# Key features as weights: two heads a product in 64-column array tiles

## The chip, the cores and the metric

The kernel runs on one core of a Trainium2 chip. The metric is the time of one execution on the device in microseconds, as the median of several runs. Before the change it is 507.56 us (three runs, 507.46 to 507.66).

## What is computed

The reference mixes two branches over one input x of 2048 rows and 512 columns:

```python
g = _sigmoid((x * gate_w).sum(-1, keepdims=True))
a = _A_ref(x, A_wqkv, A_w_phi, A_wo)
b = _B_ref(x, B_w1, B_b1, B_w2, B_b2)
return g * a + (1 - g) * b
```

Branch B is a dense layer of 1792 hidden columns with a squared ReLU. Branch A is linear attention with 32 heads of 16 columns:

```python
pq = jnp.einsum("bhsd,hdf->bhsf", q, w_phi)
pk = jnp.einsum("bhsd,hdf->bhsf", k, w_phi)
phi_q = jnp.concatenate([_softmax(pq, axis=-1), _softmax(-pq, axis=-1)], axis=-1)
phi_k = jnp.concatenate([_softmax(pk, axis=-1), _softmax(-pk, axis=-1)], axis=-1)
kv = jnp.einsum("bhsf,bhsd->bhfd", phi_k, v)
z  = jnp.einsum("bhsf->bhf", phi_k)
num = jnp.einsum("bhqf,bhfd->bhqd", phi_q, kv)
den = jnp.einsum("bhqf,bhf->bhq", phi_q, z)[..., None] + 1e-6
o = num / den
```

For each head the 2048 rows of 32 key features (16 of a softmax and 16 of the softmax of the negative) are multiplied with 16 columns of values. That gives a 32 x 16 matrix kv and a sum z of 32 numbers a head.

## The kernel before

**Order of the work.** The program goes through a list of 56 hidden steps: two sweeps over the hidden columns, in each four blocks of 512 rows, in each seven groups of 128 hidden columns. One step multiplies up (tile u), squares on ScalarE, and multiplies down (tile d). The attention is hung between these steps: `at(slot, f)` puts a piece of work at a place written out by hand, and `run(slot)` issues it there. Each engine works through its own instructions in order, so the slots set the order on TensorE and, with a few priorities (`high_priority`), on the others. Most products are done as three float32r products of high and low parts (`mm3`); the products of this change are plain float32.

**Keys and values.** In the first sweep, `tiles_fold` multiplies the key weights with w_phi (PSUM tiles fold), turns the result with four VectorE transposes (line 194, tile turned) and spreads it with 16 ScalarE copies (line 198) into the tiles raw. From these, `joint` makes the operands of a block product that yields keys and values of two row chunks (a pair) at a time, in the PSUM tiles pX and pY (lines 653 to 655). The key part becomes the features phi (tile e or tmp, 32 heads x 32 features); the value part goes into vext, where each head has 17 columns: 16 values and a one. The column of ones makes the sum z beside kv.

**The key-value products.** For each chunk of 128 rows `kv_chunk` (lines 319 to 326) issues 32 products, one a head. The weights are the 17 columns of vext, the moving side the 32 features of the head. Head 8j + g is written to the 17 partitions from 32j on, in the 32 columns from 32g on, of the one PSUM tile kvps: four array tiles of 32 columns work side by side. All 16 chunks add up in kvps. Each of eight pairs issues its two chunks in one go (`kv`, line 710).

**The end of the sums.** `kv_done` copies the four groups of 17 partitions into a zeroed tile (line 751). The row of ones lies in partitions 16, 48, 80 and 112 of it; one DMA writes these four rows to memory (zrow, line 752), two read them back into every partition (z, line 755). `kv_blocks` transposes the tile on VectorE (line 760) and copies the blocks into kvb (line 764), the weights of the numerator products num (line 385). The tile z is read by GpSimd in `q_exps` (line 333) for the denominator. The PSUM bank of kvps is handed back at the end of `kv_done`.

The queries follow in the second sweep: their weights are folded (foldq, line 152), q is projected and turned to features, and num and the output product att come after.

Of the kernel before, what the change touches and what calls it, by code (L numbers as in the profile page):

```python
# [7 lines left out]
F32 = mybir.dt.float32  # L8
F32R = mybir.dt.float32r
AF = mybir.ActivationFunctionType  # L10
# [5 lines left out]
P = 128  # L16
S, D, H, DH, F = 2048, 512, 32, 16, 1792
NK = D // P
SB = 512
NB = S // SB  # L20
# [5 lines left out]
NG = 8  # L26
VW = DH + 1
# [7 lines left out]
def tile_gated_mix(ctx: ExitStack, tc: tile.TileContext, xT, xn, wqT, wkT, wphi, wv, wo, w1, b1, w2, b2, gw, out):  # L35
    nc = tc.nc
# [6 lines left out]
    work = pool("work", 2)  # L43
    small = pool("small", 3)
    dram = pool("dram", 1, space=DRAM)
    ps_d = pool("ps_d", NC, space=PSUM)
    ps_a, ps_b, ps_e, ps_f = (pool(f"ps_{i}", 1, space=PSUM) for i in "abef")
# [5 lines left out]
    def bank(name):  # L53
        p = banks[0]
        used(p)
        return p.tile([P, 512], F32, tag="s", name=name)
# [63 lines left out]
    st, up_w, down_w = {}, {}, {}  # L120
# [6 lines left out]
    kvb = const.tile([P, NG, 2 * DH], F32, name="kvb")  # L127
# [1 line left out]
    nc.gpsimd.tensor_tensor(kvb, kvb, kvb, ALU.add)  # L129
    part = dram.tile([NB * NC, P, D], F32, name="part")  # L130
    wkeep = dram.tile([len(KEPT), 2, P, 2 * D], F32, name="wkeep")
    zrow = dram.tile([2 * D], F32, name="zrow")
    vext = [hold.tile([P, H * VW], F32, tag="vz", name=f"vext{i}") for i in range(NV)]
    heads = lambda v: v.rearrange("p (h v) -> p h v", v=VW)
    for v in vext:
# [39 lines left out]
    def tiles_fold(loaded):  # L175
        wph, *t = loaded
        pss = [bank(f"fold{r}") for r in range(4)]

        def mm(g, r, c):
            rows, cols = slice(32 * r, 32 * r + 32), slice(32 * c, 32 * c + 32)  # L180
            return nc.tensor.matmul(pss[r][cols, g * P:(g + 1) * P],
                                    wph[rows, g * P + 32 * r:g * P + 32 * r + 32],
                                    t[g][rows, :].rearrange("p (k c q) -> p k c q", c=4, q=32)[:, :, c, :],
                                    start=True, stop=True, skip_group_check=True)

        last = None
        for x in [(g, r, c) for g in range(NK) for c in range(4) for r in range(4)]:
            with tc.issue_after(last.ins) if last else nullcontext():
                last = mm(*x)
        for half in range(2):  # L190
            tb = work.tile([P, 2, 4, NK, 32], F32, tag="tb", name="turned", bufs=2)
            for r in range(2):
                with tc.high_priority(offset=AHEAD):
                    st["turned"] = nc.vector.transpose(tb[:, r].rearrange("p g k q -> p (g k q)"), pss[2 * half + r])
            for k in range(NK):
                dst = st["raw"][k].rearrange("p (h z g r f) -> p h z g r f", h=2, z=2, g=2, r=4)
                for h in range(2):
                    nc.scalar.activation(dst[:, h, 0, :, 2 * half:2 * half + 2],
                                         tb[:, :, 2 * h:2 * h + 2, k].rearrange("p r g q -> p g r q"), AF.Copy)

    def operand(i, j, src, slot=None, ehi=None, elo=None):
        if i in HELD:
# [114 lines left out]


    def kv_chunk(first, last, kvps, phi, v):
        for g in range(NG):  # L320
            for j in range(4):
                h = NG * j + g
                mm = nc.tensor.matmul(kvps[32 * j:32 * j + VW, 32 * g:32 * g + 32], v[:, h * VW:(h + 1) * VW],
                                      phi[:, 32 * h:32 * h + 32], start=(first and g == 0), stop=last,
                                      skip_group_check=True)
        return mm

    def q_exps(n, ps):
# [268 lines left out]
    LASTP = len(ROWS) - 1  # L597
# [59 lines left out]
    def pair_steps(p, s):  # L657
        b, c = ROWS[p]
        n, m = b * NC + c, b * NC + c + 2
        v = {}  # L660

        def place(t, half, src, other=None):
            i = 2 * p + (t == m)
            if ("e", t) not in v:
                v["e", t] = e_tile("tmp" if i % NV == NV - 1 else "e")
                v["v", t] = vext[i % NV]
            hs = slice(16 * half, 16 * half + 16)
            to = (v["e", t][:, hs, 0, :], heads(v["v", t])[:, hs, :DH])
            for o, cols in zip(to, halves):
                of = lambda z: z[:, cols].rearrange("p (h f) -> p h f", f=DH)  # L670
                if other is None:
                    read = nc.scalar.activation(o, of(src), AF.Copy)
                else:
                    read = nc.vector.tensor_tensor(o, of(other), of(src), ALU.add)
            return read

        def run(i):
            first, other = i in (1, 2, 7), "Y" if i in (2, 7, 4) else "X"
            if i == 1:
                if p == 0:  # L680
                    banks.remove(ps_e)
                v["X"] = ps_e.tile([P, 512], F32, tag="s", name="pX")
            elif first:
                v["bank"] = banks[0]
                v["Y"] = bank("pY")
            elif i == 4:
                used(v["bank"])
            block(v[other], p, i, first)
            with tc.high_priority(offset=AHEAD), again(p, i, 0):
                if i in (1, 6, 5):  # L690
                    v[i] = st["tmp"][0][:, 512 * (i == 6):512 * (i == 6) + 512]
                    read = nc.scalar.activation(v[i], v["X"], AF.Copy)  # L692
                elif i == 7:
                    return
                else:
                    t, half, u = {2: (n, 0, 1), 3: (n, 1, None), 4: (m, 0, 6)}[i]
                    read = place(t, half, v[other], v.get(u))
            with tc.issue_after(read.ins):
                again(p, i, 1)

        def place7():
            with tc.high_priority(offset=AHEAD):
                place(m, 1, v["Y"], v[5])

        def phi(t):
            e3, r = exps(e=v["e", t])
            with tc.high_priority(offset=AHEAD):
                v["phi", t] = scaled(e3, r)

        def kv():  # L710
            if p == 0:
                st["kv"] = ps_b.tile([P, 2 * P], F32, tag="s", name="kvps")
            later = kv_chunk(p == 0, False, st["kv"], v["phi", m], v["v", m])
            with tc.issue_after(later.ins):
                kv_chunk(False, p == LASTP, st["kv"], v["phi", n], v["v", n])

        at(s - 2 - (p > 0), sums_load, p)
        if p == 0:
            at(s - 2, sums_add, p)
        at(s - 1.5 if p else s - 0.5, sums, p)  # L720
        for off, i in zip((0, 1, 1.5, 2, 2.5, 3, 4), (1, 2, 6, 5, 7, 3, 4)):
            at(s + off, run, i)
        if p == LASTP:
            at(s + 4, banks.append, ps_e)
        at(s + 3, place7)
        at(s + 3, phi, n)
        at(s + 4, phi, m)
        at(s + 7.5 + (p == LASTP) / 2, kv)

    def do_q(b, n, c):  # L730
# [10 lines left out]

    def kv_room():
        t = row()
        st["kvs"], st["kvt"] = t[:, :2 * P], t[:, 2 * P:]
        nc.gpsimd.memset(st["kvs"], 0.0)

    def kv_done():
        kvps, kvs = st["kv"], st["kvs"]
        for j in range(4):
            s = slice(32 * j, 32 * j + VW)  # L750
            nc.vector.tensor_copy(kvs[s, :], kvps[s, :])
        nc.sync.dma_start(zrow.rearrange("(j x) -> j x", j=4), kvs[DH::32, :])
        for half in range(2):
            z = hold.tile([P, H * VW], F32, tag="vz", name=f"z{half}")[:, :D]
            nc.sync.dma_start(z, zrow[half * D:(half + 1) * D].partition_broadcast(P))
            zbc.append(z.rearrange("p (h f) -> p h f", f=DH))
        banks.append(ps_b)

    def kv_blocks():
        nc.vector.transpose(st["kvt"], st["kvs"])  # L760
        kt = st["kvt"].rearrange("p (g v) -> p g v", v=32)
        for j in range(4):
            s = slice(32 * j, 32 * j + 32)
            nc.vector.tensor_copy(kvb[s, :, DH * (j % 2):DH * (j % 2 + 1)], kt[s, :, :DH])

    def finish(n, c):
        ps = attended(st["o", n // 2], n % 2, st["wb"])
# [14 lines left out]
    SL = 2 * NFH  # L782
    steps = {}

    def at(slot, f, *a):
        steps.setdefault(int(2 * slot) / 2, []).append(lambda: f(*a))
# [10 lines left out]
    for b in range(NB):  # L797
        for c in range(NC):
            s = b * SL + 2.5 * c - 1 if b > 1 else 17.5 + c / 2 if b else max(5.5, 3.5 + 2 * c)
# [5 lines left out]
        s, late = ((4, 2), (19.5, 1), (22, 2.5), (36, 2))[b]  # L805
# [15 lines left out]
            at(slot + 1.5, ffn_split, nm, NFH + i)  # L821
    at(51, kv_room)
    at(NB * SL - 1, kv_done)
    at(NB * SL + 4, kv_blocks)

    for p in range(NB * NC // 2):
        n, s = 2 * p, 56.5 + 6 * p
        q, late = divmod(n, NC)[0], p == NB * NC // 2 - 1  # L830
# [13 lines left out]
    hid, last = {}, len(work_list) - 1  # L844
# [25 lines left out]
    for t, (sw, b, i) in enumerate(work_list):  # L870
# [17 lines left out]
        for c in range(NC):  # L888
            n = b * NC + c
# [9 lines left out]
            dst = part[n] if sw == 0 else out[n * P:(n + 1) * P, :]  # L899
# [52 lines left out]
```

## Time and profile before

| what | value |
|---|---|
| median of three runs | 507.56 us |
| profiled execution | 507.18 us |
| its span | 505.4 us |
| TensorE busy | 500.7 us, 3520 products |
| TensorE weight loads | 406.1 us |
| VectorE, ScalarE, GpSimd busy | 407.0, 256.6, 87.3 us |
| moved by DMA | 76.13 MB |

The span runs from the first to the last instruction of the profiled execution; 1.8 us of its time lie around it. PE is TensorE, PEld its weight loads, which overlap PE; DVE is VectorE, ACT ScalarE, POOL GpSimd, SP the engine that issues most DMAs. A row of a group of instructions begins with the line of the kernel, the engine and the operation, then the output tile and the inputs. For a product follow the size of the weights (rows*columns) and the size of the moving side. A busy share of PE is no measure of its peak: consecutive products overlap, and their ends are modelled.

### The profile page before, as it was taken

What the parts mean: (1) busy time and instruction counts of PE and PEld (TensorE: products, weight loads), DVE (VectorE), ACT (ScalarE), POOL (GpSimd) and SP (SyncE); (2) the same over time, 40 slices, a digit from 0 to 9 for tenths busy, and PEclk for the clock granted to TensorE, in tenths of its full rate; (3) what the DMA queues carried; (4) which work ended last, traced back from release to release, by engine and by line L of the source; (5) the groups of instructions that cost most, each with busy time, mean ns of one, the idle gap of its engine ahead of it and who ended that gap; (6) DMA issues with size and microseconds to landing.
All of it is one profiled execution on the core that took longest, in us unless ns stands there. A gap on an engine that the chain in (4) does not pass through costs nothing.

```text
span 505.4 us, 9354 instructions
## 1 busy us (share of the span) xinstructions
PE 500.7 (99%) x3520; PEld 406.1 (80%) x3520; DVE 407.0 (81%) x680; ACT 256.6 (51%) x458; POOL 87.3 (17%) x102
## 2 busy tenths in 40 slices
PE   9999999999999999999999999999999999999997
PEld 5878888788888888888888878788787878788776
DVE  5569957988695979796998989897979796897724
ACT  4887655565253474454674744454455353333540
POOL 1000151204410035000013040212222221112200
PEclk9999999999999999999999999999999999999999
DMA  8858587756854578771265311325112231041112
GB/s 261 291 196 273 198 305 225 237 190 234 285 184 165 183 223 294 265 228 65 83 211 209 98 49 48 99 64 150 49 31 90 71 86 43 8 131 57 38 27 83
DMA packets 45829, 76.13 MB, mean 151 GB/s; under 512 B 6868, under 2 KB 23000, under 8 KB 45784
## 3 DMA queue, kind: packets, MB, share of 16 engines
q1 hardware_dynamic: 36072, 41.78, 26.6%
q10 hardware_dynamic: 6768, 23.79, 13.7%
q0 software_dynamic: 2944, 9.96, 5.5%
q8 instruction: 28, 0.46, 0.4%
q14 instruction: 17, 0.14, 0.1%
HBM read 57.68 MB, written 11.54 MB: 137 GB/s over the span
## 4 chain that ended last, share of the span: by engine, by line
PE 98%; DMA 1%; DVE 0%; issue 0%
PE d L76 10%; PE d L77 10%; PE d L78 10%; PE u L76 10%; PE u L77 9%; PE u L78 9%; PE pX L653 3%; PE q L77 3%; PE att L77 3%; PE att L78 3%; PE att L76 3%; PE q L78 3%; PE q L76 3%; PE pX L655 3%; PE pX L654 3%; PE pY L655 2%
## 5 line engine op out<-in xcount | busy, mean ns | idle before, releaser
L421 ACT ACTIVATE r<-u,b1c 128x512 f32<-128x512 f32 x56 | 38.5, 687 | 122.9 <-PE u L78 121.2
L76 PE MATMUL d<-w2h,hh 128*128 128x512 f32 x222 | 86.9, 391 | 0.0
L77 PE MATMUL d<-w2l,hh 128*128 128x512 f32 x222 | 86.4, 389 | 0.0
L78 PE MATMUL d<-w2h,hl 128*128 128x512 f32 x222 | 86.4, 389 | 0.0
L76 PE MATMUL u<-xh,w1h 128*128 128x512 f32 x212 | 83.6, 394 | 0.0
L77 PE MATMUL u<-xl,w1h 128*128 128x512 f32 x212 | 82.6, 390 | 0.0
L78 PE MATMUL u<-xh,w1l 128*128 128x512 f32 x212 | 82.5, 389 | 0.0
L333 POOL TENSOR_TENSOR ez<-e,z 128x512 f32<-128x512 f32 x32 | 42.9, 1360 | 165.0 <-ACT e L309 165.0
L66 DVE TENSOR_TENSOR hl<-r,hh 128x512 fp32r<-128x512 f32 x56 | 37.8, 676 | 24.3 <-ACT hh L63 24.1
L76 PEld LDWEIGHTS d<-w2h,hh 128*128 128x128 f32 x222 | 41.7, 188 | 9.2 <-issue 0.6
L76 PEld LDWEIGHTS u<-xh,w1h 128*128 128x128 f32 x212 | 39.8, 188 | 11.1 <-issue 2.9
L78 PEld LDWEIGHTS d<-w2h,hl 128*128 128x128 f32 x222 | 41.7, 188 | 8.7
L77 PEld LDWEIGHTS d<-w2l,hh 128*128 128x128 f32 x222 | 41.7, 188 | 8.5
L78 PEld LDWEIGHTS u<-xh,w1l 128*128 128x128 f32 x212 | 39.8, 188 | 8.6 <-DVE w1l L66 0.2
L77 PEld LDWEIGHTS u<-xl,w1h 128*128 128x128 f32 x212 | 39.8, 188 | 7.9
L309 ACT ACTIVATE e<-e 128x1024 f32<-128x1024 f32 x27 | 28.6, 1059 | 26.5 <-DVE e L307 26.1
L291 DVE TENSOR_REDUCE sm<-e 128x64 f32<-128x1024 f32 x27 | 32.8, 1215 | 10.8 <-ACT e L309 10.8
L63 ACT ACTIVATE hh<-r 128x512 fp32r<-128x512 f32 x56 | 35.2, 628 | 1.1
L423 ACT ACTIVATE r<-r 128x512 f32<-128x512 f32 x56 | 34.9, 624 | 0.7
L692 ACT ACTIVATE tmp<-pX 128x512 f32<-128x512 f32 x24 | 14.4, 598 | 30.6 <-PE pX L655 27.0
L374 ACT ACTIVATE phiT<-tb 32x256 f32<-32x256 f32 x64 | 26.4, 412 | 5.8 <-DVE tb L359 4.9
L343 DVE TENSOR_REDUCE dz<-ez 128x64 f32<-128x1024 f32 x16 | 19.4, 1212 | 11.7 <-POOL ez L333 11.7
(182 smaller groups left out, 984.2 us busy)
## 6 DMA issues: line engine op xcount, KB each, us to landing
sloto<-wkeep ACTq DMA_DIRECT2D x30, 512.0 KB, 4.6
in<-in_xT SPq DMA_DIRECT2D x42, 256.0 KB, 4.4
slotez<-wkeep ACTq DMA_DIRECT2D x15, 512.0 KB, 5.0
phiT<-tb SPq DMA_DIRECT2D x192, 32.0 KB, 1.8
in<-in_w SPq DMA_DIRECT2D x23, 256.0 KB, 3.3
part<-row POOLq DMA_DIRECT2D x16, 256.0 KB, 5.5
row<-part SPq DMA_DIRECT2D x16, 256.0 KB, 3.0
out<-row SPq DMA_DIRECT2D x15, 256.0 KB, 2.2
```

The costliest lines, as they stand in the source:

```text
L63: i = nc.scalar.activation(hi, src, AF.Copy)
L66: st["lo"] = elo.tensor_tensor(lo, src, hi.bitcast(F32), ALU.subtract)
L76: nc.tensor.matmul(o, ah[:, sa], bh[:, sb], start=first, stop=False)
L77: nc.tensor.matmul(o, ah[:, sa], bl[:, sb], start=False, stop=False)
L78: return nc.tensor.matmul(o, al[:, sa], bh[:, sb], start=False, stop=last)
L291: nc.vector.tensor_reduce(sm, e3, AX.X, ALU.add)
L309: nc.scalar.activation(ef, ef, AF.Exp)
L333: nc.gpsimd.tensor_tensor(ez[:, hs, :], e3[:, hs, :], zbc[half], ALU.mult)
L374: nc.scalar.activation(dst, src, AF.Copy)
L421: st["relu"] = nc.scalar.activation(r, ps, AF.Relu, bias=b1c[:, fc:fc + 1])
L423: nc.scalar.activation(r, r, AF.Square)
L655: nc.tensor.matmul(ps, l, wh, start=False, stop=j == 1, skip_group_check=True)
```

## The change

The two sides of the key-value product are exchanged, and two heads share a product. The weights are now 64 columns: the features of two heads. The moving side is the extended values of the same two heads, 2 x 17 columns. The product has four blocks, of which the two with features and values of the same head are used. It is written to 64 partitions of kvps, so that two array tiles of 64 columns take turns.

```diff
     def kv_chunk(first, last, kvps, phi, v):
+        fs = phi.rearrange("p (q g f) -> q g p f", q=2, g=NG)
+        vs = v.rearrange("p (q a g f) -> q g p a f", q=2, a=2, g=NG)
         for g in range(NG):
-            for j in range(4):
-                h = NG * j + g
-                mm = nc.tensor.matmul(kvps[32 * j:32 * j + VW, 32 * g:32 * g + 32], v[:, h * VW:(h + 1) * VW],
-                                      phi[:, 32 * h:32 * h + 32], start=(first and g == 0), stop=last,
-                                      skip_group_check=True)
+            for q in range(2):
+                mm = nc.tensor.matmul(kvps[64 * q:64 * q + 64, 2 * VW * g:2 * VW * (g + 1)], fs[q, g], vs[q, g],
+                                      start=(first and g == 0), stop=last, skip_group_check=True)
         return mm
```

For this the features of the two heads must lie side by side. The order of the key columns is changed where the folded weights are spread; the values stay where they were:

```diff
-            tb = work.tile([P, 2, 4, NK, 32], F32, tag="tb", name="turned", bufs=2)
+            tb = work.tile([P, NK, 4, 2, 32], F32, tag="tb", name="turned", bufs=2)
             for r in range(2):
                 with tc.high_priority(offset=AHEAD):
-                    st["turned"] = nc.vector.transpose(tb[:, r].rearrange("p g k q -> p (g k q)"), pss[2 * half + r])
+                    st["turned"] = nc.vector.transpose(tb[:, :, :, r].rearrange("p k g q -> p g k q"),
+                                                       pss[2 * half + r].rearrange("p (g k q) -> p g k q", g=4, k=NK))
             for k in range(NK):
-                dst = st["raw"][k].rearrange("p (h z g r f) -> p h z g r f", h=2, z=2, g=2, r=4)
+                dst = st["raw"][k].rearrange("p (h z i a d) -> p h z a i d", h=2, z=2, i=NG, a=2)
                 for h in range(2):
-                    nc.scalar.activation(dst[:, h, 0, :, 2 * half:2 * half + 2],
-                                         tb[:, :, 2 * h:2 * h + 2, k].rearrange("p r g q -> p g r q"), AF.Copy)
+                    nc.scalar.activation(dst[:, h, 0, :, 4 * half:4 * half + 4],
+                                         tb[:, k, 2 * h:2 * h + 2].rearrange("p a r (i d) -> p a (r i) d", i=2),
+                                         AF.Copy)
```

The sums now have the features on the partitions, as kvb needs them. They are copied straight from PSUM into the blocks, and only the column of sums, 8 of 32 columns, is transposed on its way to zrow; `kv_blocks` is gone:

```diff
     def kv_done():
-        kvps, kvs = st["kv"], st["kvs"]
-        for j in range(4):
-            s = slice(32 * j, 32 * j + VW)
-            nc.vector.tensor_copy(kvs[s, :], kvps[s, :])
-        nc.sync.dma_start(zrow.rearrange("(j x) -> j x", j=4), kvs[DH::32, :])
+        kv = st["kv"]
+        blocks = [(slice(32 * j, 32 * j + 32), j % 2) for j in range(4)]
+        for s, a in blocks:
+            nc.vector.tensor_copy(st["z"][s, :NG], kv[s, :, a, DH])
+        nc.vector.transpose(st["zt"], st["z"])
+        nc.sync.dma_start(zrow.rearrange("(p f) -> p f", f=32), st["zt"])
+        for s, a in blocks:
+            nc.vector.tensor_copy(kvb[s, :, DH * a:DH * (a + 1)], kv[s, :, a, :DH])
+        zr = zrow.rearrange("(j g f) -> j (g f)", j=4, f=32)
         for half in range(2):
             z = hold.tile([P, H * VW], F32, tag="vz", name=f"z{half}")[:, :D]
-            nc.sync.dma_start(z, zrow[half * D:(half + 1) * D].partition_broadcast(P))
+            nc.sync.dma_start(z.rearrange("p (j x) -> p j x", j=2),
+                              zr[2 * half:2 * half + 2, :32 * NG].partition_broadcast(P))
             zbc.append(z.rearrange("p (h f) -> p h f", f=DH))
         banks.append(ps_b)
-
-    def kv_blocks():
-        nc.vector.transpose(st["kvt"], st["kvs"])
-        kt = st["kvt"].rearrange("p (g v) -> p g v", v=32)
-        for j in range(4):
-            s = slice(32 * j, 32 * j + 32)
-            nc.vector.tensor_copy(kvb[s, :, DH * (j % 2):DH * (j % 2 + 1)], kt[s, :, :DH])
```

The rest follows from it: kvps is declared as 8 x 2 x 17 columns, zrow grows from 1024 to 4096 numbers, and the zeroed tile shrinks from 256 to 32 columns.

More of the change, by code (lines that the diff above doesn't have):

```diff
@@ L131, in tile_gated_mix @@
     wkeep = dram.tile([len(KEPT), 2, P, 2 * D], F32, name="wkeep")
-    zrow = dram.tile([2 * D], F32, name="zrow")
+    zrow = dram.tile([P * 32], F32, name="zrow")
     vext = [hold.tile([P, H * VW], F32, tag="vz", name=f"vext{i}") for i in range(NV)]
@@ L711, in kv @@
             if p == 0:
-                st["kv"] = ps_b.tile([P, 2 * P], F32, tag="s", name="kvps")
-            later = kv_chunk(p == 0, False, st["kv"], v["phi", m], v["v", m])
+                st["kv"] = ps_b.tile([P, NG, 2, VW], F32, tag="s", name="kvps")
+            out = st["kv"].rearrange("p g a v -> p (g a v)")
+            later = kv_chunk(p == 0, False, out, v["phi", m], v["v", m])
             with tc.issue_after(later.ins):
-                kv_chunk(False, p == LASTP, st["kv"], v["phi", n], v["v", n])
+                kv_chunk(False, p == LASTP, out, v["phi", n], v["v", n])
         at(s - 2 - (p > 0), sums_load, p)
@@ L743, in kv_room @@
         t = row()
-        st["kvs"], st["kvt"] = t[:, :2 * P], t[:, 2 * P:]
-        nc.gpsimd.memset(st["kvs"], 0.0)
+        st["z"], st["zt"] = t[:, :32], t[:, 32:64]
+        nc.gpsimd.memset(st["z"], 0.0)
     def kv_done():
-        kvps, kvs = st["kv"], st["kvs"]
-        for j in range(4):
-            s = slice(32 * j, 32 * j + VW)
-            nc.vector.tensor_copy(kvs[s, :], kvps[s, :])
-        nc.sync.dma_start(zrow.rearrange("(j x) -> j x", j=4), kvs[DH::32, :])
+        kv = st["kv"]
[7 more added lines that the diff above has]
+        zr = zrow.rearrange("(j g f) -> j (g f)", j=4, f=32)
         for half in range(2):
             z = hold.tile([P, H * VW], F32, tag="vz", name=f"z{half}")[:, :D]
-            nc.sync.dma_start(z, zrow[half * D:(half + 1) * D].partition_broadcast(P))
+            nc.sync.dma_start(z.rearrange("p (j x) -> p j x", j=2),
+                              zr[2 * half:2 * half + 2, :32 * NG].partition_broadcast(P))
             zbc.append(z.rearrange("p (h f) -> p h f", f=DH))
         banks.append(ps_b)
-    def kv_blocks():
-        nc.vector.transpose(st["kvt"], st["kvs"])
-        kt = st["kvt"].rearrange("p (g v) -> p g v", v=32)
-        for j in range(4):
-            s = slice(32 * j, 32 * j + 32)
-            nc.vector.tensor_copy(kvb[s, :, DH * (j % 2):DH * (j % 2 + 1)], kt[s, :, :DH])
     def finish(n, c):
@@ L823, in tile_gated_mix @@
     at(NB * SL - 1, kv_done)
-    at(NB * SL + 4, kv_blocks)
     for p in range(NB * NC // 2):
```

## The prediction

> **What bounds the kernel now.** I read the page first: the share of each engine, the slices and the chain that ended last.
>
> ```profile
> span 505.4 us, 9354 instructions
> ...
> PE 500.7 (99%) x3520; PEld 406.1 (80%) x3520; DVE 407.0 (81%) x680; ACT 256.6 (51%) x458; POOL 87.3 (17%) x102
> ...
> PE   9999999999999999999999999999999999999997
> ...
> PEclk9999999999999999999999999999999999999999
> ...
> PE 98%; DMA 1%; DVE 0%; issue 0%
> ```
>
> PE is busy in 500.7 of 505.4 us, no slice of it is open, its clock is granted in full, and 98% of the chain that ended last lies on it. The waits of PE are the second view; this is all of it:
>
> ```profile
> PE warm L497 <- DVE zeros L491: 1.2, 1, 1.2
> PE pX L653 <- DMA sloto<-wkeep: 0.2, 1, 0.2
> ```
>
> PE waits for 1.4 us in the run, 1.2 of it at the start. So a change is worth what it does to PE's own stream, and work on the other engines is covered as long as it ends before PE asks for it. The stream that changes is the key-value products of line 323. The timeline of PE and of its weight loads (PEld) around the first pair of chunks:
>
> ```profile
> 88.45 0.39 PE L78 MATMUL d<-w2h,hl 128*128 128x512 f32 x1
> 88.77 1.17 PEld L323 LDWEIGHTS kvps<-e,vext 128*17 128x17 f32 x128 [0.35 <-issue]
> 88.77 1.29 PE L323 MATMUL kvps<-e,vext 128*17 128x32 f32 x128
> ...
> 89.99 0.19 PEld L653 LDWEIGHTS pX<-sloto,sh 128*128 128x128 f32 x1
> 89.99 0.50 PE L653 MATMUL pX<-sloto,sh 128*128 128x512 f32 x1
> 90.10 0.19 PEld L654 LDWEIGHTS pX<-sloto,sh 128*128 128x128 f32 x1
> ```
>
> Columns: start, duration, engine, line. A pair of chunks holds 64 products in the code and 128 records: an fp32 product shows twice, each time with a load of its own. From its first start to the start of the next foreign product pass 89.99 - 88.77 = 1.22 us. The windows view, restricted to the tile kvps, gives the eight pairs (first and last row of eight, and the sum; second and third number are PE and PEld):
>
> ```profile
> 88.00:91.00 3.00, 1.29 (x128) 1.17 (x128) 0.00 (x0) 1.00 0.70 246
> ...
> 246.00:249.00 3.00, 1.29 (x128) 1.17 (x128) 0.00 (x0) 1.00 0.18 51
> sum 24.00, PE 10.23 PEld 9.27 DVE 0.00; mean PE 1.28 PEld 1.16 DVE 0.00
> ```
>
> PE's mean is 10.23/8 = 1.28, 0.01 under the first pair, so a pair holds PE for 1.21 us, and all eight for 9.7 us, 1.9% of the span. More than that the change cannot win.
>
> **What sets the 1.21 us.** Loads start (1.17 - 0.10)/127 = 8.4 ns apart, 17 ns a product. What loads and products cost by size is read from forms that stand elsewhere (minimum, median and maximum; partitions times elements at the end):
>
> ```profile
> L323 PEld LDWEIGHTS kvps<-e,vext x704: 92/97/98, 88.8 to 247.6; 128*17 128x17 f32 x176
> L323 PE MATMUL kvps<-e,vext x704: 193/193/205, 88.8 to 247.6; 128*17 128x32 f32 x176
> L181 PE MATMUL fold<-row x128: 265/268/292, 26.5 to 28.1; 32*32 32x128 f32 x128
> L385 PE MATMUL num<-phiT,kvb x256: 376/376/400, 297.5 to 489.2; 64*32 64x256 f32 x128
> L653 PE MATMUL pX<-sloto,sh x16: 389/390/499, 58.5 to 229.6; 128*128 128x512 f32 x16
> ...
> 244.71 1.05 PE L152 MATMUL foldq<-row 128*128 128x128 f32 x8
> ...
> 244.48 1.08 PEld L152 LDWEIGHTS foldq<-row 128*128 128x128 f32 x8
> ...
> 26.46 1.63 PEld L181 LDWEIGHTS fold<-row 32*32 32x32 f32 x128 [0.35 <-issue]
> ```
>
> The longest record of each form is a first one, which could not hide its load: 205 - 193 = 12 ns for 17 weight columns, 292 - 268 = 24 and 400 - 376 = 24 for 32, 499 - 389 = 110 for 128. The last figure stands in the timeline too: after the pair, the second load starts at 90.10, 0.11 us behind the first. So a load holds its array tile for some 0.7 to 0.86 ns a column, whatever the rows. The stream of foldq shows that loads of 128 columns run beside products: (1.05 - 0.27)/7 = 111 ns a record, with a load of 110 in it. It prices an fp32 pass at no more than 111/128 = 0.87 ns a moving column. And tiles load side by side: 128 loads of 24 ns, 3.1 us, start within 1.63 us in the fold; 128 of 12 ns, 1.54 us, within 1.17 us here.
>
> For one pair before, three limits: issue, 64 products at 17 ns, 1.09 us; products, 32 records in each of four column tiles x 32 columns x 0.87, 0.89 us; loads, 32 x 12, 0.38 us. Issue decides; with 0.12 us from the last start to the next foreign one it makes the 1.21.
>
> **The change, part by part.** *Products.* A pair issues 32 products, 64 records, in place of 64 and 128. The weights are now 64 columns of key features (v's 17 before), the moving side 2 x 17 = 34 columns of v, in two column tiles. The same limits: issue 32 x 17 = 0.54 us; products, 32 records a tile x 34 x 0.87 = 0.95 us; loads, 32 a tile of 64 columns each. No row shows a load of 64 columns. Bounds from the nearest rows: twice the 24 of 32 columns, 48, and half the 110 of 128 columns, 55; the straight line between them gives 24 + 86/3 = 53, which I take. Loads: 32 x 53 = 1.70 us. They outlast the products that would hide them (30 ns each), so **the weight load becomes the limit**: 1.70 + 0.12 = 1.82 us a pair, 0.61 more than now, 8 x 0.61 = +4.9 us. With 48 it is 1.66 us and +3.6; with 56 (110 plus a start of 2 ns, halved) 1.91 us and +5.6. The order, column tile 0 and 1 by turns, lets the two load side by side. The 0.35 us of idle loads ahead of the stream, marked issue, stays: the array's tiling still changes there.
>
> The Trainium skill, page "TensorE: Matmul & The Clock Gate", section "The mechanism" in Part 3, speaks against this sum: a load overlaps running products only where the row groups differ, and here each product takes all rows. The foldq rows (all 128 rows, 111 ns for a load of 110 and its product) contradict it for the untiled array; what it would make of the tiled one is the third rival.
>
> *Fold.* The four transposes write with other strides, and 16 ACT copies read and write the same 128 x 128 in runs of 16 instead of 64 elements.
>
> ```profile
> L194 DVE STREAM_TRANSPOSE turned<-fold 128x512 f32<-128x512 f32 x4 | 2.5, 685 | 0.4 <-PE fold L181 0.4
> L198 ACT ACTIVATE tmp<-turned 128x128 f32<-128x128 f32 x8 | 2.1, 295 | 0.0
> ...
> L653 PE MATMUL pX<-sloto,xh x16: 389/389/499, 51.8 to 214.0; 128*128 128x512 f32 x16
> ...
> 32.00:40.00 8.00, 8.00 (x35) 6.24 (x35) 5.56 (x10) 7.25 (x18) 1.24 (x2) 1.00 0.64 201
> ```
>
> Same counts and sizes, so I take 0; if the strides doubled both, it were 2.7 us of DVE and some 4.7 of ACT near 30 us, and PE first uses what comes of it at 51.8; in the window after 32 us (columns: length, PE, PEld, DVE, ACT) DVE is free for 2.4 of 8 us and ACT for 0.8, and more lies between 40 and 51.8. Without that cover the 4.7 would be PE's.
>
> *End of the sums.*
>
> ```profile
> L751 DVE COPY row<-kvps 17x256 f32<-17x256 f32 x4 | 1.7, 419 | 0.1
> L760 DVE STREAM_TRANSPOSE row<-row 128x256 f32<-128x256 f32 x1 | 0.4, 448 | 0.0
> L764 DVE COPY kvb<-row 32x128 f32<-32x128 f32 x4 | 0.9, 219 | 0.1
> ...
> 255.08 0.62 SPq L752 DMA_DIRECT2D zrow<-row  x1
> 257.81 0.84 SPq L755 DMA_DIRECT2D z<-zrow  x2
> DMA to landing us min/median/max: 4.7/4.8/4.9
> 267.15 2.55 POOL L333 TENSOR_TENSOR ez<-e,z 128x512 f32<-128x512 f32 x2 [2.96 <-ACT e L309]
> ```
>
> Removed: 1.7 + 0.4 + 0.9 = 3.0 us of DVE. Added: four copies of 32 x 8 and four of 32 x 128 (at most 219 to 419 each), and a transpose of 128 x 32 (at most 448): 2 to 3 us. Net 0 to -1 us, beside PE. One DMA writes the sums in 128 rows of 128 B instead of four of 1 KB, two read them in two pieces a partition. SP holds the first until the transpose is done and the two until it has landed; behind them in its queue stand loads of w2 and x, which waited in the same way before. They land near 258.3 + 4.8 = 263.1, and POOL first uses them at 267.15, held by ACT: 4 us of room. If both took twice as long, POOL would start some microseconds late, but PE's first product out of this (num) is at 297.5. I count 0; without cover the delay would be PE's.
>
> Sum: the profiled execution took 507.18 us (span 505.4, 1.8 around it), the median of the runs is 507.56. 507.18 + 4.9 = 512.1; on the median 512.5, which I give.
>
> **The rivals.** *Half the products, half the time* (the other side). If loads and products of the two tiles stay under the issue rate, a pair takes 0.54 + 0.12 = 0.66 us, and the kernel 507.56 - 8 x 0.55 = 503.2. For it: the stream of now is issue-bound. Against it: a load of 64 columns had to hold its tile for 17 ns, and 32 columns took 24. The Trainium skill, page "TensorEngine Tiling (Array Packing)", section "Instruction Overhead", leans this way: short products cost by their number, not their width.
>
> *Products bind:* loads faster than I take them, 30 ns or less a tile: 0.95 + 0.12 = 1.07 us, -0.14 a pair, 506.4. The same row of 32 columns speaks against it.
>
> *Load and product one after the other in a tile:* 32 x (53 + 30) = 2.66 + 0.12 us, +1.57 a pair, 520.1. Against it: in this way a pair took 32 x (12 + 28) = 1.28 us before, with its tail 1.40, and it took 1.21.
>
> *One load at a time for both tiles:* 64 x 53 = 3.39 + 0.12 us, +2.3 a pair, 526. Against it stand the 128 loads of 24 ns in 1.63 us.
>
> **How the numbers follow.** Loads bind, side by side: 0.70, from 511.1 (48 ns) to 513.2 (56 ns). Issue binds: 0.11. Products bind: 0.09. One after the other: 0.06. One load at a time: 0.04. A measurement of this kernel tells 0.2%, 1 us, from no change; the products' case (-1.2 us) lies on that edge and I split it: faster 0.11 + 0.045, same 0.045, slower 0.80. The range takes in the likeliest case and the products' one, 506.4; upward it goes to 515, where each load loses 10 ns of its overlap (32 x 10 ns x 8 = 2.6 us); with these partial losses it holds 8 in 10.
>
> **What would show it.** Right: kvps loads of 64 columns x64 a pair, some 135 ns long in the record (between the 97 of 17 columns and the 0.19 us of 128), starting 26 to 28 ns apart on the mean, 1.8 us from the first to the next foreign start, PE still without waits, and every other stretch between pairs as long as before. Wrong: starts 8 ns apart (issue), 15 (products), 42 (one after the other), 53 (one at a time); or a wait on PE behind the fold or before num.

## The result and the profile after

The changed kernel takes 513.13 us in the median of four runs (513.01 to 513.59), against 507.51 us before (four runs, 507.41 to 507.66). The ratio is 1.0112 with a 95% interval of 1.0099 to 1.0125: **slower by 5.6 us**. The profiled execution took 513.59 us.

The page of the changed kernel, shares of the engines and slices of PE:

```profile
span 511.8 us, 8326 instructions
...
PE 507.0 (99%) x3008; PEld 412.2 (81%) x3008; DVE 405.6 (79%) x680; ACT 255.8 (50%) x458; POOL 86.9 (17%) x102
...
PE   8999999999999999999999999999999999999997
```

There are 512 product records fewer (3008 for 3520), and TensorE is busy 6.3 us longer. PE waits for 1.4 us, as before. All its waits are these:

```profile
PE warm L499 <- DVE zeros L493: 1.2, 1, 1.2
PE fold L181 <- issue: 0.2, 1, 0.2
```

So the time is in the stream of products itself. The timeline of the changed kernel around the first pair of chunks, with the next foreign product behind it:

```profile
89.47 1.95 PEld L326 LDWEIGHTS kvps<-vext,e 128*64 128x64 f32 x64 [0.35 <-issue]
89.47 2.06 PE L326 MATMUL kvps<-vext,e 128*64 128x34 f32 x64
...
91.46 0.19 PEld L655 LDWEIGHTS pX<-sloto,sh 128*128 128x128 f32 x1
91.47 0.50 PE L655 MATMUL pX<-sloto,sh 128*128 128x512 f32 x1
91.57 0.19 PEld L656 LDWEIGHTS pX<-sloto,sh 128*128 128x128 f32 x1
```

A pair holds TensorE from 89.47 to 91.47, 1.99 to 2.00 us; it was 1.21. The windows view, restricted to kvps (first and last row of eight, and the sum), shows the same in every pair:

```profile
89.00:92.00 3.00, 2.06 (x64) 1.95 (x64) 0.00 (x0) 1.00 0.67 223
...
252.00:255.00 3.00, 2.06 (x64) 1.95 (x64) 0.00 (x0) 1.00 0.17 38
sum 24.00, PE 16.48 PEld 15.58 DVE 0.00; mean PE 2.06 PEld 1.95 DVE 0.00
```

Eight pairs cost 8 x (1.99 - 1.21) = 6.2 us more. The loads are fewer by half, 64 for 128, and take 1.95 us for 1.17. One load of the record:

```profile
L326 PEld LDWEIGHTS kvps<-vext,e x352: 132/138/138, 89.5 to 253.6; 128*64 128x64 f32 x176
L326 PE MATMUL kvps<-vext,e x352: 224/224/245, 89.5 to 253.6; 128*64 128x34 f32 x176
```

From the first load's start to the last one's are 1.95 - 0.14 = 1.81 us for 63 steps: 28.7 ns a record, **57.5 ns for two**. As two array tiles take turns, each tile starts a load every 57.5 ns on the mean.

The other parts of the change do what they were counted at. The four transposes of the fold (first row below) take as long as before, and so do the 16 copies behind them, 294 ns each. At the end of the sums the VectorE groups of the changed kernel are the other two:

```profile
L194 DVE STREAM_TRANSPOSE turned<-fold 128x512 f32<-128x512 f32 x4 | 2.5, 684 | 0.9 <-PE fold L181 0.9
...
L758 DVE COPY kvb<-kvps 32x128 f32<-32x128 f32 x4 | 1.1, 286 | 0.1
...
L754 DVE COPY row<-kvps 32x8 f32<-32x8 f32 x4 | 0.6, 160 | 0.0
```

With a transpose of 0.20 us that makes 1.9 us for the 3.0 us of before. The two reads of z are issued at 263.74 and take longer, up to 6.7 us for up to 4.9 before. GpSimd still does not wait for them but for ScalarE (the timeline of SP, z's time to landing, and the timeline of POOL):

```profile
263.74 0.89 SPq L762 DMA_DIRECT2D z<-zrow  x2
...
DMA to landing us min/median/max: 5.3/6.0/6.7
...
273.57 2.53 POOL L335 TENSOR_TENSOR ez<-e,z 128x512 f32<-128x512 f32 x2 [3.58 <-ACT e L311]
```

### The profile page after: what moved, and what is told of

Read it like the earlier page. It is cut to its first block, busy times and chain, and to the rows that moved or that the text cites. A ratio compares the mean times of both kernels' runs of the same rounds, so it can differ in the third digit from the quotient of the medians.

```text
span 511.8 us, 8326 instructions
## 1 busy us (share of the span) xinstructions
PE 507.0 (99%) x3008; PEld 412.2 (81%) x3008; DVE 405.6 (79%) x680; ACT 255.8 (50%) x458; POOL 86.9 (17%) x102
## 4 chain that ended last, share of the span: by engine, by line
PE 98%; DMA 1%; SPq 0%; ACT 0%; issue 0%; DVE 0%
PE d L76 10%; PE d L77 10%; PE d L78 10%; PE u L76 10%; PE u L77 9%; PE u L78 9%; PE pX L655 3%; PE kvps L326 3%; PE pX L657 3%; PE pX L656 3%; PE q L77 3%; PE att L77 3%; PE att L78 3%; PE att L76 3%; PE q L78 3%; PE q L76 3%
```

## The experiments

The theory: a load of n weight columns holds its array tile for a time that grows with n, and the next load in the same tile starts only after that time. (The records of loads are longer, 0.14 us, and overlap; the hold is read from the step between their starts.) With 64 columns this is longer than the product beside it. The strongest rival came up only with the result: if the products of the two tiles ran one after the other, 34 moving columns at the prediction's bound of 0.87 ns, 30 ns a record at most, would give about the same 58 ns for two. Two more: that part of the 5.6 us comes from the other edits, and that load and product add up within a tile. The edits below are made to `kv_chunk` of the changed kernel; each diff shows the lines that count, and `...` stands for what is left out of them. Where the output loses heads, the copies at the end read from what is there. The first experiment has twelve runs, from 506.9 to 508.7 us; each of the others is a single execution, so its pairs of chunks say more than its total.

**One head a product again** (e1_one_head).

```diff
-        fs = phi.rearrange("p (q g f) -> q g p f", q=2, g=NG)
+        fs = phi.rearrange("p (q g a f) -> q g p a f", q=2, g=NG, a=2)
...
-            for q in range(2):
-                mm = nc.tensor.matmul(kvps[64 * q:64 * q + 64, 2 * VW * g:2 * VW * (g + 1)], fs[q, g], vs[q, g],
+            for j in range(4):
+                q, a = divmod(j, 2)
+                c = VW * (2 * g + a)
+                mm = nc.tensor.matmul(kvps[32 * j:32 * j + 32, c:c + VW], fs[q, g][:, a],
+                                      vs[q, g][:, a], ...
```

> The changed kernel with its products alone taken back to one head each: 32 weight columns of key features, 17 moving columns of values, four 32-column array tiles; fold, end of the sums and output as in the changed kernel. Theory (the weight load holds its tile for about 0.83 ns a column + 5): loads 32 x 32 ns = 1.0 us a pair, under the issue of 64 products x 17 ns = 1.09, so a pair takes 1.2 us as before the change and the kernel 507.0 to 507.9 us. Rival (part of the 5.6 us comes from the fold's new copies or the end of the sums): over 508.5.

It took 507.46 us, beside 507.75 for the kernel before on the same chip; the ratio is 1.0001 with an interval of 0.9993 to 1.0010. The first pair in its timeline:

```profile
89.84 1.30 PE L328 MATMUL kvps<-vext,e 128*32 128x17 f32 x128
91.06 0.51 PE L657 MATMUL pX<-sloto,sh 128*128 128x512 f32 x1
...
89.83 1.20 PEld L328 LDWEIGHTS kvps<-vext,e 128*32 128x32 f32 x128 [0.35 <-issue]
```

91.06 - 89.84 = 1.22 us, as before the change. Everything else of the change is still in this kernel: the new order of the keys, the exchange of weights and moving side, the shorter end. All of it together is worth nothing that can be measured: the interval leaves about half a microsecond at most to either side. So the loss lies in putting two heads into one product.

**Half the moving side** (e2_moving17).

```diff
-  ... kvps[64 * q:64 * q + 64, 2 * VW * g:2 * VW * (g + 1)], fs[q, g], vs[q, g],
+  ... kvps[64 * q:64 * q + 64, 2 * VW * g:2 * VW * g + VW], fs[q, g], vs[q, g][:, 0],
```

> The changed kernel with the moving side halved: the values of the first head of the two alone, 17 columns; the second head's sums are copied from the first's columns. Theory (load of 64 columns binds): starts stay 58 ns apart for each two records, a pair stays at 1.95 to 2.0 us, 513.1 us. Rival (the products of the two tiles run one after the other, 34 columns x 0.83 = 28 ns + 1 each, which gives the same 58 ns for two): 2 x 15 ns for two records, 1.1 us a pair, 506 us.

```profile
90.14 2.05 PE L326 MATMUL kvps<-vext,e 128*64 128x17 f32 x64
92.12 0.50 PE L655 MATMUL pX<-sloto,sh 128*128 128x512 f32 x1
...
90.14 1.95 PEld L326 LDWEIGHTS kvps<-vext,e 128*64 128x64 f32 x64 [0.35 <-issue]
```

The timeline of this run has half the moving columns (128x17) and the same 1.95 us of loads and 1.98 us a pair. The moving side does not set the time with 34 columns, and the rival that gave the same 58 ns by chance is out. The kernel took 514.37 us, 1.2 more than expected, but not in the pairs: all eight take 15.8 us together, and 15.9 in the changed kernel. Outside of the pairs the spans of the eleven profiles lie between 495.5 and 496.8 us, and this run is at the upper end.

**Half the weights** (e3_weights32) **and three quarters** (e5_weights48).

```diff
-  ... kvps[64 * q:64 * q + 64, 2 * VW * g:2 * VW * (g + 1)], fs[q, g], vs[q, g],
+  ... kvps[64 * q:64 * q + 32, 2 * VW * g:2 * VW * (g + 1)], fs[q, g][:, :32], vs[q, g],
```

The second has 48 in both places.

> The changed kernel with the weights halved: the features of the first head of the two alone, 32 of 64 columns, moving side as it is with 34; the second head's sums are copied from the first's rows. Theory (load binds): load 32 ns and product 33 ns in each tile, 33 to 34 ns for two records, 1.2 us a pair, 506.9 us. Rival (products one after the other): 58 ns for two records as in the changed kernel, 513 us.

> The changed kernel with 48 of the 64 weight columns of each product: the features of the first head and half of the second's; the second head's sums are copied from the first's rows. Theory (a load holds its tile for a part that goes with its columns, and a small fixed one): halfway between the 32.4 ns of 32 columns and the 58.4 ns of 64, 45 to 46 ns for two records, 1.43 us from first to last start, 1.58 us a pair. Rival (the load goes in steps of a whole 64-column tile as soon as it is over 32): 58 ns as with 64.

Timeline of the first, then of the second:

```profile
89.35 1.22 PE L326 MATMUL kvps<-vext,e 128*32 128x34 f32 x64
90.50 0.50 PE L655 MATMUL pX<-sloto,sh 128*128 128x512 f32 x1
...
89.35 1.10 PEld L326 LDWEIGHTS kvps<-vext,e 128*32 128x32 f32 x64 [0.35 <-issue]
```

```profile
89.49 1.63 PE L326 MATMUL kvps<-vext,e 128*48 128x34 f32 x64
91.06 0.50 PE L655 MATMUL pX<-sloto,sh 128*128 128x512 f32 x1
...
89.49 1.52 PEld L326 LDWEIGHTS kvps<-vext,e 128*48 128x48 f32 x64 [0.35 <-issue]
```

With a last load of 0.11 and 0.125 us taken off, two records take 31.4 ns with 32 columns, 44.3 with 48 and 57.5 with 64: from step to step 0.81 and 0.83 ns for each weight column more, with some 5 ns that do not go with the columns. A pair takes 1.15, 1.57 and 1.99 us, and the kernels 506.87, 510.25 and 513.13. The time follows the weights' columns in a straight line; there is no step to a full tile. In the first of the two, 34 moving columns are about as long as the load, so its 31.4 ns may belong to either. The number of products is the same in all three, so their issue does not set these times.

**More moving columns** (e6_moving60, e7_moving96).

```diff
-  ... kvps[64 * q:64 * q + 64, 2 * VW * g:2 * VW * (g + 1)], fs[q, g], vs[q, g],
+  c = 2 * VW * g + 200 * q
+  ... kvps[64 * q:64 * q + 64, 60 * g:60 * g + 60], fs[q, g], v[:, c:c + 60],
```

The PSUM tile is declared 512 columns wide for this. The second run writes 96 columns from 96 * (g % 5) on. Neither keeps the sums of the heads.

> The changed kernel with 60 moving columns in each product instead of 34: neighbouring value columns, written to a wider piece of the same PSUM bank; its sums are not those of the heads. Theory (load and product run side by side, the longer one binds): product 60 x 0.83 + 5 = 55 ns, under the load, so 58 ns for two records and 1.84 us from first to last start as in the changed kernel. Rival (part of the product lies behind the load): 58 ns grows by some of the 22 ns that the product grew, up to 80.

> The same with 96 moving columns (pieces of the PSUM bank are written by several products); its sums are not those of the heads. Theory: now the product binds, 96 x 0.83 + 5 = 85 ns for two records, 2.7 us from first to last start. Rival (load and product add up): 58 + 80 = 138 ns.

Timeline of the run with 60 columns, then of that with 96:

```profile
88.88 2.08 PE L327 MATMUL kvps<-vext,e 128*64 128x60 f32 x64
90.89 0.50 PE L656 MATMUL pX<-sloto,sh 128*128 128x512 f32 x1
...
88.88 1.95 PEld L327 LDWEIGHTS kvps<-vext,e 128*64 128x64 f32 x64 [0.35 <-issue]
```

```profile
89.95 2.87 PE L327 MATMUL kvps<-vext,e 128*64 128x96 f32 x64
92.75 0.50 PE L656 MATMUL pX<-sloto,sh 128*128 128x512 f32 x1
...
89.95 2.68 PEld L327 LDWEIGHTS kvps<-vext,e 128*64 128x64 f32 x64 [0.35 <-issue]
```

With 60 moving columns the loads still take 1.95 us and the kernel 513.33 us: 26 columns more in every product cost nothing, since they lie beside the load. With 96 the products are the longer side: (2.68 - 0.14)/63 x 2 = 81 ns for two records, or 0.84 ns for each of the 96 columns; a pair takes 2.80 us and the kernel 520.52. Load and product do not add up, which would have given 138 ns. The longer of the two binds.

**One tile after the other** (e4_tile_by_tile).

```diff
-        for g in range(NG):
-            for q in range(2):
+        for q in range(2):
+            for g in range(NG):
```

> The changed kernel with the order of a chunk's 16 products changed: eight of the first column tile, then eight of the second. Theory (a tile's next load waits for the tile, and the two tiles load side by side only because they take turns): 58 ns for one record, 3.75 us a pair, +1.8 x 8: 527 us; if loads of the second tile are pulled ahead over eight products, unchanged at 513. Rival (products one after the other): unchanged.

```profile
90.27 3.30 PE L326 MATMUL kvps<-vext,e 128*64 128x34 f32 x64
93.50 0.50 PE L655 MATMUL pX<-sloto,sh 128*128 128x512 f32 x1
...
90.27 3.19 PEld L326 LDWEIGHTS kvps<-vext,e 128*64 128x64 f32 x64 [0.35 <-issue]
```

The same 64 records take 3.23 us a pair, and the kernel 524.38 us, 11 us more for the order of a loop: 8 x (3.23 - 1.99) = 9.9 us in the pairs, and 1.8 us in waits of PE for ScalarE that the changed kernel's profile does not have. A record takes (3.19 - 0.14)/63 = 48 ns on the mean, between the 29 of tiles that take turns and the 58 of a single tile. The expectation had the two ends, 527 us and 513 us; the run lies near the first. The trace shows what is between them. The windows view of kvps has two stretches of 0.30 us, one within the first tile's records and one where the order changes tile (the second bracket counts the loads that run in the stretch):

```profile
90.60:90.90 0.30, 0.30 (x9) 0.30 (x7) 0.00 (x0) 1.00 0.60 220
90.90:91.20 0.30, 0.30 (x13) 0.30 (x11) 0.00 (x0) 1.00 0.47 164
```

By the starts of the single loads, those of one tile follow each other every 58 ns, and only the eight around each change of tile every 32 ns (260 ns for eight, then 467 for the next eight, in all pairs alike). So one tile alone needs 58 ns a load, two load side by side, and where the order changes tile some loads of the second run ahead beside the last ones of the first.

**Both kernels once more** (before_again, after_again). In the first profile of the changed kernel the stream of the fold, whose products are not changed, was 0.6 us longer than before: a gap stands ahead of its last six loads. The loads of the fold in the changed kernel's timeline:

```profile
26.56 1.59 PEld L181 LDWEIGHTS fold<-row 32*32 32x32 f32 x122 [0.35 <-issue]
28.63 0.14 PEld L181 LDWEIGHTS fold<-row 32*32 32x32 f32 x6 [0.48 <-issue]
```

> The kernel before the change, profiled on this chip beside the other runs. Theory: a pair of chunks holds TensorE for 1.20 to 1.23 us; the fold's stream of 128 records lasts 1.83 us as in the first profile, or now and then 0.6 us longer as in the profile of the changed kernel, which would make that stretch no part of the change. Rival: it is 1.83 us whenever the key columns keep their old order.

> The changed kernel, profiled once more. Theory: eight pairs of 1.99 us, 58 ns for two records, as in its first profile; the fold's stream, which lasted 1.83 us in the kernel before and 2.41 us in the first profile of the changed one, differs from execution to execution (1.83 to 2.49 us in the six experiments that share its code) and may come out anywhere between. Rival: it is 2.4 us in the changed kernel every time.

The same loads in the second profile of the changed kernel:

```profile
26.72 1.64 PEld L181 LDWEIGHTS fold<-row 32*32 32x32 f32 x128 [0.35 <-issue]
```

The stream is whole again, 1.83 us to the next product as in both profiles of the kernel before. So the gap comes and goes in one and the same kernel and is no fixed part of the change. Of the experiments' profiles two have it too (e2_moving17 and e5_weights48, ahead of the same load). The trace points to a cause: in these three executions a packet of 16 KB in the DMA queue that the page marks "instruction" started only 0.2 to 0.5 us before the stream, in all others 0.9 us or more, and the first load behind the gap came 2.33 us after that packet's start each time. So the stream seems to wait for its own instructions; no run varied this. The pairs are the same to 0.01 us in both profiles of each kernel. The two new executions took 507.11 and 513.87 us.

No version among these beats the kernel before. The run with 32 weight columns and 34 moving ones (506.87 us) leaves out half of the heads' products.

## Why the prediction was right

The prediction was 512.5 us, on the grounds that the weight load becomes the limit; the result is 513.13 us.

- *TensorE is the only bound, and nothing takes over.* Right. PE waits as little as before, although VectorE now waits longer for the products of the pairs (10.6 us in all, 3.3 before). 8 x 0.78 = 6.2 us of longer pairs stand beside a span that grew by 6.4 us.
- *Half the products do not halve the time.* Right, and shown: the limit moved from issue (17 ns a product) to the load. The rival in which issue binds is refuted by e3_weights32 and e5_weights48: with the same number of products, fewer weight columns alone make the pairs shorter. The rival in which the products bind is refuted by e2_moving17, where 17 moving columns are no faster than 34.
- *Loads and products side by side.* Right: e6_moving60. With it falls the rival of 520 us. The rule of the Trainium skill, page "TensorE: Matmul & The Clock Gate", Part 3, "The mechanism", by which a load overlaps running products only where the row groups differ, does not hold here as it stands (the section itself excepts loads into a background weight buffer, which no run here can show). Every product takes all rows, and 60 moving columns leave the 57.5 ns of a load as they are.
- *The two tiles load side by side.* Right: 28.7 ns a record in place of the 58 of one tile, and e4_tile_by_tile shows what is lost without it. With it falls the rival of 526 us.
- *The size of the load.* The mechanism was right and this term too small. I took 53 ns for 64 columns, with 48 and 56 as ends; it is 57.5, outside both. From the first product's start to the last one's pass 1.84 us for the 1.70 counted, and behind it 0.15 us for 0.12: 8 x 0.17 = 1.4 us, about the 1.3 by which 4.9 fell short of 6.2.
- *The way to that size* does not hold, and that it came so near is in part luck. I read the load from the time by which a first product is late, 24 ns for 32 columns. The products' records with 64 weight columns in the changed kernel (shown above) are late by 245 - 224 = 21 ns, and with 48 weight columns, then with 64 and 96 moving ones, they read:

```profile
L326 PE MATMUL kvps<-vext,e x352: 211/211/232, 89.5 to 250.5; 128*48 128x34 f32 x176
L327 PE MATMUL kvps<-vext,e x352: 244/246/297, 90.0 to 260.1; 128*64 128x96 f32 x176
```

  That is 21 ns again for 48 columns, and 51 for the same 64: the delay does not follow the weights' columns, so in these streams it is no measure of the load. The other source, the stream of foldq, was the better one: its 111 ns a record for 128 columns lie on the line of the experiments (128 x 0.83 + 5 = 111), though load and product are about equally long there. What counts in a stream is the step from load to load.
- *Fold and end of the sums at nothing.* Right, by e1_one_head. (The copies do not read in runs of 16, as the prediction has it: they read one run of 128 and write runs of 16. They take no longer for it.) The reads of z became slower by up to 1.8 us, inside the 4 us of room.
- The medians differ by 5.6 us, the eight pairs by 6.2. Single executions of one kernel differ by some tenths and more (513.0 to 513.9 here, 506.9 to 508.7 in e1_one_head), and the interval of the ratio reaches from 5.0 to 6.3 us, so what lies between the two stays open. The first profile of the changed kernel has 0.6 us of the fold's gap in its span besides.

## What to carry to other kernels

In a stream of small products count three things: the issue by the number of products, and for each array tile the load by the columns of the weights and the product by the moving columns. Take the longest. Beside one head a product (as in e1_one_head), two heads in one halve the first and double the other two in each tile. Before you halve a count, find out how far the next limit is away: in that kernel the load stood at 1.0 us (32 x 31.4 ns) beside 1.09 of issue. Read the load from the step between starts in a stream that it binds, not from the delay of a first product. Let neighbouring products use different array tiles, since the order of one loop alone cost 9.9 us in the pairs.

## What the runs showed of the hardware

- The step from load to load in one column tile has some 5 ns that do not go with the columns (31.4, 44.3 and 57.5 ns for 32, 48 and 64). The delay of a first product does not show the load: it is 21 ns with 48 and with 64 weight columns, and 51 with 64 and a longer moving side.
- Where the order passes from one column tile to the other only after eight products, the loads still overlap in part: eight loads around each change of tile follow every 32 ns, the others every 58.
- The fold's stream of 128 loads broke off ahead of its last records in three of eleven profiled executions and took 0.4 to 0.7 us longer, with no wait in the profile. In all three a packet of the instruction queue had started later than in the other eight. I had not expected that from an unchanged stream.
